# A written start-up order for fused attention and feed-forward: two rows of six sequences in the second tile, and GpSimd as a third engine in the weights' conversion

## The chip, the cores and the metric

The kernel runs on one core of a Trainium2 chip. The metric is the device time of one execution in microseconds (us). The core has a matrix engine (TensorE, PE in the profile, its weight loads PEld), VectorE (DVE), ScalarE (ACT), GpSimd (POOL) and SyncE (SP), whose queue issues the DMAs here.

## The reference

Eight sequences of 576 tokens go through attention with eight heads of 64 channels, and the joined heads through a feed-forward layer. Four heads see the last 32 tokens (local), the other four see every 32nd token before their own (strided).

```python
scores = scale * np.matmul(q, k.transpose(0, 1, 3, 2))
mask_local = (rel >= 0) & (rel < stride)
mask_strided = (rel >= 0) & (pos[None, :] % stride == pos[:, None] % stride)
attn = np.exp(scores - max); attn = attn / (sum + 1e-09)
x = matmul(attn, v)                      # (4608 tokens, 512)
h = x @ w_in                             # 512 -> 2048
return (0.5 * h * (1.0 + erf(h * inv_sqrt2))) @ w_out   # 2048 -> 512
```

## The kernel before, in words

**Tiles and steps.** The 4608 tokens are twelve tiles of 384 tokens, that is twelve rows of 32 tokens each. VISITS (L39) lists in which order rows of which sequence fill the tiles: an entry is (sequence, first row, last row). Tile 0 is rows 0 to 11 of sequence 0; tile 1 is rows 0 to 3 of sequences 1, 2 and 3. For each tile the feed-forward part has sixteen steps, one for each block of 128 hidden channels: ffn_h (L614) multiplies x by the block of w_in, twelve matmuls into H; ffn_g (L624) takes Gelu on ScalarE, rounds the result to a high part gh on ScalarE and forms the rest gl on VectorE; ffn_o (L647) multiplies by the block of w_out, nine matmuls into three accumulators O. Each product is computed as three, from operands split into a high and a low part: xh and xl, gh and gl, and the two halves of w. Steps 0 to 15 are tile 0, step 16 is the first of tile 1; there are 192.

**Weights.** Each of the 16 blocks of both weight matrices arrives as 64-bit numbers and is converted once (split_w, L141), in five instructions of 128x1024 elements, each of which may stand elsewhere in the order: the leading bits to a buffer lead (L154 on VectorE for the weights in TOP_V, L156 on ScalarE for the others), these as an integer word (L159, ScalarE), shift and OR with the rest (L161, VectorE), the high part (L165 on VectorE for those in HIGH_V, L167 on ScalarE), and the low part by subtraction (L169, VectorE). There is one buffer lead. Weights and staging share 17 slots of one pool, and a load waits until the third load before it has landed (L136).

**Local heads.** A job is 128 tokens of four heads; three jobs fill a tile. The first three jobs (local_job, L240) use dense masks; each quotient stands on VectorE (L229) for the jobs in QUOT_V and on ScalarE (L232) for the other. All others are band jobs (band_job, L282): scores (L297, 32 matmuls), maximum (L311), exponential (L315), sum and quotient and a 32x32 transpose (L318 to L321), eight DMAs of 16 KB into a band tile (L326), values (L337, 16 matmuls), and the split into xh (L236) and xl (L238).

**Strided heads.** Tile 0's strided part is done with matmuls: half_tile (two halves a and b, L375) and strided_tile (A, L418). Its operands are loaded by S and B (load_a L357, load_b L370); load_a also clears a tile p on GpSimd (L363), into which VectorE then writes. For all later tiles VectorE does it in pairs of a query row and a key row, in units of up to four rows: one L494 for each score, one L534 or L536 for each weighted value, and eight instructions for each unit (L502, L503, L520, L526, L527, L524, the transpose L544 and the split L238), besides one exponential on ScalarE (L504) and a clearing of the scores on GpSimd (L487). Tile 1 has 30 pairs in three units. load_strided (L459) loads q, k and v of a group of visits; here the three sequences of tile 1 are three DMAs each.

**What sets the order.** START (L48) is a written order up to the steady part. An entry is a job and stands for its next part: c is a weight's conversion (five parts), f a step (H, Gelu, gh, gl, O), L a local job (eleven parts, band jobs seven), a, b and A the strided part of tile 0, u1 that of tile 1 in groups of eight instructions; w, q, v, S, B, E and e are loads. Within START (L780) VectorE, ScalarE, TensorE and SP follow the written order:

```python
    with tc.manual_schedule(engines={ET.DVE, ET.Activation, ET.PE, ET.SP}):
        for it in START:
```

GpSimd's order is left to the framework's scheduler, here and later. In the steady part step(n) (L850) writes one step after the other, and run_strided (L688) deals out VectorE's strided work by a running sum of costs (0.137 a score, 0.196 a value, 0.6 a unit's end) against the due time of each tile. At thirteen steps into a tile there is a visit (L829): the values of the next tile's three band jobs (48 matmuls L337) and then the scores of the three jobs of the tile after that (96 matmuls L297), in one go. Nine visits have both, those with the values of tiles 2 to 10:

```python
    FIRST, VISIT = 2, 13
    value_at = {ready[t - 1] + VISIT: t for t in range(2, NTILE)}
    score_at = {ready[1] + FIRST: 2, **{n: t + 1 for n, t in value_at.items()}}
```

Before START, GpSimd builds the masks (mask, mask0, three masks bmask for the band jobs, L720 to L737), an identity and three cleared band tiles (L746).

Of the kernel before, what the change touches and what calls it, by code (L numbers as in the profile page):

```python
# [82 lines left out]
def attn_ffn_kernel(ctx: ExitStack, tc: tile.TileContext, qk, vl, qka, va, qs, ks, vs, w, out):  # L83
# [30 lines left out]
    smask = const.tile([P, MA], F32, name="smask")  # L114
    mask = const.tile([P, LK], F32, name="mask")
    mask0 = const.tile([P, LK], F32, name="mask0")

    bmask = {i: const.tile([P, 2 * STRIDE], F32, name=f"bmask{i}") for i in (None, 0, 1)}
# [830 lines left out]
```

## Time and profile before

| what | value |
|---|---|
| median of 3 runs | 876.04 us (874.67 to 878.77) |
| the profiled execution, own time | 877.5 us |
| its span, first to last instruction | 875.7 us |
| TensorE busy | 856.4 us (98%) |
| VectorE busy | 706.2 us (81%) |
| ScalarE busy | 482.7 us (55%) |
| GpSimd busy | 17.5 us (2%) |
| DMA | 66.67 MB, 76 GB/s in the mean |
| mean granted TensorE clock | 0.990 of full speed |

The profile is of one execution. Busy time of TensorE counts overlapping matmuls as one stretch, so what it lacks to 100% is time in which no matmul ran; the granted clock says at which share of its full speed TensorE was let run. Time lines count from the first instruction. In a time line a row gives start, length, engine, line, operation, output and inputs, and in brackets the idle time of the engine before it with what ended that; rows with a count (x) join neighbours of one kind.

### The profile page before, as it was taken

To read this page: it belongs to the slowest core of one execution; us is meant where nothing else is said; L and a number is where in the kernel's file an instruction comes from. 1 tells how busy PE (TensorE), PEld (TensorE's weight loads), DVE (VectorE), ACT (ScalarE), POOL (GpSimd) and SP (SyncE) were. 2 spreads that over 40 slices of the span, in tenths; PEclk is the share of its full clock that TensorE was granted. 3 is DMA by queue.
4 is the path that set the end of the run, shared out by engine and by line. 5 is a ranking of instruction groups with operands and counts; after the bars stand their busy time and mean duration, and the time that the engine had idled before them with its cause. 6 is when DMAs were issued, how large, how long until landed. Compare 5 with 4: busy or idle time off the path is not lost.

```text
span 875.7 us, 19634 instructions
## 1 busy us (share of the span) xinstructions
PE 856.4 (98%) x6082; PEld 771.0 (88%) x6082; DVE 706.2 (81%) x4901; ACT 482.7 (55%) x1001; POOL 17.5 (2%) x89
## 2 busy tenths in 40 slices
PE   5999999999999999999999999999999989999998
PEld 4888898999999999999999899989989979989997
DVE  6998999998989997889999979899799993751111
ACT  7888585566465375357355445556547435443222
POOL 5000100000000000000000000000000000000000
PEclk9799999999999999999999999999999999999999
DMA  9695301320310320310311121131032002000001
GB/s 352 223 380 200 115 24 37 108 76 8 128 47 9 101 97 10 104 44 8 97 50 58 55 76 47 34 122 48 9 101 80 12 30 59 18 6 12 26 1 37
DMA packets 34552, 66.67 MB, mean 76 GB/s; under 512 B 6800, under 2 KB 16528, under 8 KB 34448
## 3 DMA queue, kind: packets, MB, share of 16 engines
q1 hardware_dynamic: 34448, 65.43, 22.1%
q8 instruction: 48, 0.79, 0.4%
q14 instruction: 56, 0.46, 0.2%
HBM read 51.64 MB, written 9.44 MB: 70 GB/s over the span
## 4 chain that ended last, share of the span: by engine, by line
PE 90%; DVE 3%; DMA 3%; ACT 2%; SPq 1%; issue 1%; DVEq 0%; ACTq 0%
PE H L619 15%; PE O L659 14%; PE O L660 14%; PE H L621 14%; PE H L620 14%; PE O L658 14%; PE X_L L337 1%; PE S L297 1%; DMA ws<-in_w_dram 1%; DMA qka<-in_qka_dram 1%; DMA sk<-in_ks_dram 1%; DVE ws L161 1%; SPq L326 1%; PE S L337 1%; DVE w L169 1%
## 5 line engine op out<-in xcount | busy, mean ns | idle before, releaser
L628 ACT ACTIVATE H<-H 128x384 f32<-128x384 f32 x192 | 91.3, 476 | 363.0 <-PE H L621 304.3
L619 PE MATMUL H<-xh,w 128*128 128x384 f32 x768 | 261.6, 341 | 1.5 <-DVE gl L632 1.4
L621 PE MATMUL H<-xh,w 128*128 128x384 f32 x768 | 260.6, 339 | 0.0
L620 PE MATMUL H<-xl,w 128*128 128x384 f32 x768 | 259.4, 338 | 0.4 <-DVE xl L238 0.4
L536 DVE SCALAR_TENSOR_TENSOR acc<-sv,sc,acc 128x64 f32<-128x64 f32 x1158 | 249.5, 275 | 0.7
L660 PE MATMUL O<-w,gl 128*128 128x512 f32 x576 | 228.3, 396 | 0.0
L659 PE MATMUL O<-w,gh 128*128 128x512 f32 x576 | 227.7, 395 | 0.0
L658 PE MATMUL O<-w,gh 128*128 128x512 f32 x576 | 224.4, 390 | 0.0
L494 DVE CUSTOM_DVE_ANT_0 junk<-sq,sk 128x64 f32<-128x64 f32 x1290 | 203.8, 217 | 3.5 <-DMA sk<-in_ks_dram 2.4
L632 DVE TENSOR_TENSOR gl<-H,gh 128x384 fp32r<-128x384 f32 x192 | 105.7, 551 | 106.0 <-ACT gh L630 105.1
L619 PEld LDWEIGHTS H<-xh,w 128*128 128x128 f32 x768 | 145.4, 189 | 11.1 <-DVE gl L632 1.7
L620 PEld LDWEIGHTS H<-xl,w 128*128 128x128 f32 x768 | 145.3, 189 | 8.5 <-DVE xl L238 0.8
L621 PEld LDWEIGHTS H<-xh,w 128*128 128x128 f32 x768 | 145.0, 189 | 0.1
L660 PEld LDWEIGHTS O<-w,gl 128*128 128x128 f32 x576 | 108.1, 188 | 23.7 <-DVE gl L632 0.6
L659 PEld LDWEIGHTS O<-w,gh 128*128 128x128 f32 x576 | 108.1, 188 | 18.2
L658 PEld LDWEIGHTS O<-w,gh 128*128 128x128 f32 x576 | 108.5, 188 | 17.3
L494 DVE DVE_READ_ACCUMULATOR2_ANT sc<- 128x1 f32 x1290 | 103.6, 80 | 0.0
L630 ACT CAST gh<-H 128x384 fp32r<-128x384 f32 x192 | 92.2, 480 | 6.1
L628 ACT ACT_TABLE_LOAD x60 | 77.0, 1283 | 1.0
L504 ACT ACT_TABLE_LOAD x35 | 44.9, 1283 | 0.6
L315 ACT ACTIVATE PT_L<-P_L,nm_L 128x64 f32<-128x64 f32 x132 | 44.2, 337 | 0.3
L315 ACT ACT_TABLE_LOAD x24 | 30.8, 1283 | 0.5
(114 smaller groups left out, 488.7 us busy)
## 6 DMA issues: line engine op xcount, KB each, us to landing
ws<-in_w_dram SPq DMA_DIRECT2D x16, 1023.8 KB, 10.1
qk<-in_qk_dram SPq DMA_DIRECT2D x36, 320.0 KB, 5.0
out_dram<-ob SPq DMA_DIRECT2D x34, 256.0 KB, 2.4
vl<-in_vl_dram SPq DMA_DIRECT2D x36, 192.0 KB, 4.3
sk<-in_ks_dram SPq DMA_DIRECT2D x8, 576.0 KB, 5.5
sv<-in_vs_dram SPq DMA_DIRECT2D x8, 576.0 KB, 3.9
band<-PT_L SPq DMA_DIRECT2D x240, 16.0 KB, 1.8
sq<-in_qs_dram SPq DMA_DIRECT2D x4, 576.0 KB, 4.4
```

The costliest lines, as they stand in the source:

```text
L315: nc.scalar.activation(pv[:, :, h, :], p1[:, h * 2 * QB:(h + 1) * 2 * QB].rearrange("p (c t) -> p c t", c=2), AF.Exp, bias=nm[:, h:h + 1], ...
L494: nc.vector.tensor_tensor_reduce(junk, sq[vi, "q"][:, r0 + r, :], sq[vi, "k"][:, c, :], 1.0, 0.0, ALU.mult, ALU.add, ss[u][:, r, c:c + 1])
L536: nc.vector.scalar_tensor_tensor(acc[:, r, :], sq[vi, "v"][:, c, :], wgt, acc[:, r, :], ALU.mult, ALU.add)
L619: nc.tensor.matmul(hp, w1[f][:, 0, c, :], xh[:, c, :], start=(c == 0), stop=False)
L620: nc.tensor.matmul(hp, w1[f][:, 0, c, :], xl[:, c, :], start=False, stop=False)
L621: nc.tensor.matmul(hp, w1[f][:, 1, c, :], xh[:, c, :], start=False, stop=(c == NC - 1))
L628: nc.scalar.activation(hp, hp, AF.Gelu)
L630: nc.scalar.copy(gh, hp)
L632: nc.vector.tensor_tensor(gl, hp, gh.bitcast(F32), ALU.subtract)
L658: nc.tensor.matmul(o, gh[:, sl], w2[f][:, 0, :], start=(f == 0), stop=False)
L659: nc.tensor.matmul(o, gh[:, sl], w2[f][:, 1, :], start=False, stop=False)
L660: nc.tensor.matmul(o, gl[:, sl], w2[f][:, 0, :], start=False, stop=(f == NF - 1))
```

## The change

- VISITS: tile 1 is now rows 0 and 1 of sequences 1 to 6, two by two; sequence 7 follows whole, then rows 2 to 17 of sequences 1 to 6, then the rest of sequence 0. A unit may now hold two rows each of two sequences (units, pairs); tile 1 has 18 pairs in three units, and the tiles after it have 1272 pairs in 40 units instead of 1260 in 37.
- load_strided: a group of several sequences is one DMA for each of q, k and v. A band mask for two first rows takes the place of one of the three.
- split_w: five words (WORD_P) and five high parts (HIGH_P) go to GpSimd; VectorE takes four leading bits instead of one and three high parts instead of eight; lead has two buffers. The quotients of jobs 0 and 1 go to ScalarE (QUOT_V is empty).
- START is another order, and GpSimd follows it too.
- LATE: the scores of tiles 6 and 11 are written two steps after the visits to which they belonged.
- mask, mask0, smask and zero lie in unused columns of the slot pbig.

```diff
-VISITS = [(0, 0, 12), (1, 0, 4), (2, 0, 4), (3, 0, 4), (4, 0, 18), (5, 0, 18), (6, 0, 18), (7, 0, 18),
-          (1, 4, 18), (2, 4, 18), (3, 4, 18), (0, 12, 18)]
+VISITS = [(0, 0, 12), *[(b, 0, 2) for b in range(1, 7)], (7, 0, 18), *[(b, 2, 18) for b in range(1, 7)],
+          (0, 12, 18)]
...
 NB = 16
 START = """
-    q0 q2 S0 q1 v0 w0 B0 w1 L0 w3 L2 L0 L0 L2 L2 L0 a0 L0 L0 b0 a0 L2 a0 L0 L2 a0 L1 L2 b0 b0 b0 L0 L1
-    L2 a0 L0 b0 a0 L1 b0 a0 b0 w2 a0 b0 a0 q5 b0 L0 a0 v2 L1 L2 b0 L0 v1 c0 L1 a0 q4 L1 b0 c0 L1 A0 L1
-    c0 A0 w5 A0 c1 c0 A0 c0 c1 A0 c3 L5 c1 c3 L2 L5 L1 c2 v5 c1 w6 L4 c3 w4 L1 L2 c2 L1 L2 L4 f0 L5 w7
-    c2 L4 c1 c2 f0 f1 L5 c2 f0 c5 f0 L4 c5 f0 c3 f1 c5 f1 f2 c4 f1 c4 c5 c3 f1 f2 f2 c4 c7 L5 f2 c4 c5
-    f3 L5 w8 c7 c4 w9 E f2 f3 L5 c6 f3 c7 c6 f4 f3 c7 c6 w12 f3 c7 f4 f4 c8 c6 f5 w10 f4 c8 v3 c6 q3 w11
-    c9 c8 f4 f5 u1 f5 c9 f6 f5 w13 u1 c8 v4 c9 f5 c12 w15 c8 f6 e f6 f7 c12 u1 c9 f6 c12 f6 f7 f7 c9 w14
-    c10 f8 f7 c12 u1 c10 c12 f7 f8 c10 c11 f9 u1 c11 c10 f8 c13 c11 L4 L3 f9 f8 f9 c10 f8 c13 f9 c11 c13
-    f10 c14 c11 c14 L3 f9 c13 f10 c14 f10 L4 f11 u1 f10 c13 L3 f10 L4 u1 f11 L3 f12 u1 f11 c14 f11 u1
-    f13 f12 f12 c15 c14 f11 f13 f12 f13 u1 c15 f14 f13 u1 f12 f14 c15 f14 f14 c15 L3 u1 f13 L3 c15 u1 L3
-    f15 u1 f14 f15 f15 f15 f15 f15
+    q0 S0 q2 q1 v0 B0 w0 L0 L0 L0 b0 a0 L0 b0 L0 b0 L2 L0 a0 b0 a0 L1 b0 a0 b0 a0 L0 L2 a0 L0 b0 a0 L2
+    b0 L0 a0 b0 a0 b0 L1 v3 a0 L0 q3 b0 v1 L1 a0 w1 L2 L0 q4 c0 A0 v2 w2 L1 A0 c0 L2 w7 L1 A0 L1 c0 L2
+    L1 L3 L1 c0 A0 L2 c0 w3 L1 q5 L2 A0 c1 L2 L1 c1 L3 L2 L1 L3 L4 L2 w4 c1 e f0 c2 c1 L4 w5 c2 c1 L4 c2
+    f0 f1 w6 L3 c2 f0 L4 c3 L5 f1 f0 f1 c2 f0 c3 f1 c7 c4 c3 f2 c4 c7 c3 c4 f1 f2 c3 c4 c7 f2 f3 c5 f2
+    c4 c6 c5 f2 f3 L5 f3 c5 c6 f4 w8 f3 L5 w9 c6 w10 v4 f3 c5 c6 c5 f4 L3 c6 f5 w11 f4 L3 f4 c7 L5 f4 c8
+    c7 f5 c8 L3 f5 f6 c9 f5 c8 c9 L4 c8 f6 f7 c9 f6 L4 c10 c8 c9 f5 w12 c10 E f6 L4 w13 c11 c10 w14 f8
+    f7 c9 f7 c10 f6 f7 f8 w15 c10 f8 v5 c11 f8 f9 c12 c11 c12 f7 u1 f9 f9 c11 c12 f10 c13 f9 c11 c13 f8
+    u1 c12 f10 f10 c13 c14 f11 f10 c14 c12 f9 f11 c14 c15 c13 u1 c15 L5 f10 L5 c15 f11 u1 L5 c13 f12 f11
+    c14 u1 f11 f12 c14 u1 f13 f12 c15 f12 u1 f12 f13 f13 c15 f14 f13 u1 f13 f14 u1 f14 u1 f14 f15 u1 f14
+    f15 f15 f15 f15 f15
 """.split()
-TOP_V = [6]
-HIGH_V = [0, 1, 2, 3, 5, 6, 10, 13]
-QUOT_V = (0, 1)
+TOP_V = [0, 2, 4, 12]
+HIGH_V = [0, 5, 8]
+WORD_P = [1, 2, 5, 7, 8]
+HIGH_P = [2, 6, 9, 12, 13]
+QUOT_V = ()
...
 def units(most):
     res = []
     for k, (vi, b, r) in enumerate(ROWS):
-        if res and res[-1][0] == vi and k % TR and res[-1][3] < most:
+        n = VISITS[vi][2] if VISITS[vi][1] == 0 and VISITS[vi][2] <= most // 2 else 0
+        if res and k % TR and res[-1][3] < most and (res[-1][0] == vi or n and res[-1][6] == n):
             res[-1][3] += 1
         else:
-            res.append([vi, b, r, 1, k // TR, k % TR])
-    return res
+            res.append([vi, b, r, 1, k // TR, k % TR, n])
+    return [(*x[:6], x[6] or x[3]) for x in res]
+def pairs(u):
+    _, _, r0, nr, _, _, per = PLACE[u]
+    return [(c, r) for c in range(r0 + per) for r in range(nr) if r0 + r % per >= c]
 PLACE = units(UR)
...
         raw = wst.pop(f)
         word, other = [raw.bitcast(U32).rearrange("p (n two) -> p n two", two=2)[:, :, i] for i in range(2)]
         hf = word.bitcast(F32)
-        lead = lpool.tile([P, 2 * DM], F16, name=f"lead_{f}", tag="lead", bufs=1)
+        lead = lpool.tile([P, 2 * DM], F16, name=f"lead_{f}", tag="lead", bufs=2)
         top = raw.bitcast(BF16).rearrange("p (n four) -> p n four", four=4)[:, :, 2]
         if f in TOP_V:
             nc.vector.tensor_copy(lead, top)
...
             nc.scalar.copy(lead, top)
         yield
-        nc.scalar.activation(other.bitcast(I32), lead.bitcast(I16), AF.Copy, scale=65536.0)
+        if f in WORD_P:
+            nc.gpsimd.tensor_scalar(other.bitcast(I32), lead.bitcast(I16), 65536.0, None, ALU.mult)
+        else:
+            nc.scalar.activation(other.bitcast(I32), lead.bitcast(I16), AF.Copy, scale=65536.0)
         yield
         nc.vector.scalar_tensor_tensor(word, word, 13, other, ALU.logical_shift_right, ALU.bitwise_or)
         yield
         wt = slot(f"w_{f}", [P, 2, 2 * DM], F32R)
         if f in HIGH_V:
             nc.vector.tensor_copy(wt[:, 0, :], hf)
+        elif f in HIGH_P:
+            nc.gpsimd.tensor_copy(wt[:, 0, :], hf)
         else:
             nc.scalar.copy(wt[:, 0, :], hf)
         yield
         nc.vector.tensor_tensor(wt[:, 1, :], hf, wt[:, 0, :].bitcast(F32), ALU.subtract)
         w1[f] = wt[:, :, 0:DM].rearrange("p t (c f) -> p t c f", c=NC)
         w2[f] = wt[:, :, DM:]
+    pbig = slot("pbig", [P, 4 * DM])
+    rest = [pbig[:, i * 2 * DM + 4 * LK + DM:(i + 1) * 2 * DM] for i in range(2)]
+    pbig = [pbig[:, i * 2 * DM:(i + 1) * 2 * DM] for i in range(2)]
+    mask, mask0 = [r[:, 0:LK] for r in rest]
+    smask, zero = rest[0][:, LK:LK + MA], rest[1][:, LK:LK + 32]
     xt = {}
...
         src = {"q": qs, "k": ks, "v": vs}[nm]
         t = spool.tile([P, NR, D], F32, name=f"s{nm}_{gr}", tag=f"s{nm}", bufs=1)
         for vi in first_of[gr]:
-            b, r0, r1 = VISITS[vi]
-            o = groups[vi][1]
-            sq[vi, nm] = t[:, o:o + r1]
-            if nm != "q":
-                r0 = 0
-            nc.sync.dma_start(t[:, o + r0:o + r1], src[b, :, r0:r1])
+            sq[vi, nm] = t[:, groups[vi][1]:]
+        b, r0, r1 = VISITS[gr]
+        n = len(first_of[gr])
+        assert [VISITS[vi] for vi in first_of[gr]] == [(b + i, r0, r1) for i in range(n)] and (n == 1 or r0 == 0)
+        if nm != "q":
+            r0 = 0
+        nc.sync.dma_start(t[:, r0:n * r1].rearrange("p (b r) d -> p b (r d)", b=n),
+                          src[b:b + n, :, r0:r1].rearrange("b p r d -> p b (r d)"))
     ss = {}
     exps, splits = [], []
...
             nc.gpsimd.memset(s[:, :, 0:W], NEG)
             ss[u] = s
         ops.append((0.0, init))
-        for c in range(W):
-            for r in range(max(0, c - r0), nr):
-                def f(r=r, c=c):
-                    junk = spool.tile([P, D], F32, name=f"junk_{u}_{r}_{c}", tag="junk", bufs=4)
-                    nc.vector.tensor_tensor_reduce(
-                        junk, sq[vi, "q"][:, r0 + r, :], sq[vi, "k"][:, c, :], 1.0, 0.0,
-                        ALU.mult, ALU.add, ss[u][:, r, c:c + 1])
-                ops.append((0.137, f))
+        for c, r in pairs(u):
+            def f(r=r, c=c):
+                junk = spool.tile([P, D], F32, name=f"junk_{u}_{r}_{c}", tag="junk", bufs=4)
+                nc.vector.tensor_tensor_reduce(
+                    junk, sq[vi, "q"][:, r0 + r, :], sq[vi, "k"][:, r // per * per + c, :], 1.0, 0.0,
+                    ALU.mult, ALU.add, ss[u][:, r, c:c + 1])
+            ops.append((0.137, f))
         def sm():
             s = ss[u][:, :, 0:W]
...
     ET = mybir.EngineType
     running = {}
-    with tc.manual_schedule(engines={ET.DVE, ET.Activation, ET.PE, ET.SP}):
+    with tc.manual_schedule(engines={ET.DVE, ET.Activation, ET.PE, ET.SP, ET.Pool}):
...
-    FIRST, VISIT = 2, 13
+    FIRST, VISIT, LATE = 2, 13, (6, 11)
     value_at = {ready[t - 1] + VISIT: t for t in range(2, NTILE)}
-    score_at = {ready[1] + FIRST: 2, **{n: t + 1 for n, t in value_at.items()}}
+    score_at = {ready[1] + FIRST: 2, **{n + 2 * (t + 1 in LATE): t + 1 for n, t in value_at.items()}}
     soft_at = {}
     for n, t in score_at.items():
         for i in range(JPT if t < NTILE else 0):
...
     def visit(n):
         t = value_at.get(n, 0)
-        if score_at.get(n, 0):
-            banks[score_at[n]] = score_banks(score_at[n])
+        new = t + 1 if t else score_at.get(n, 0)
+        if new and new not in banks:
+            banks[new] = score_banks(new)
         for i in range(JPT if t else 0):
             part(t * JPT + i, 4)
         for i in range(JPT if score_at.get(n, NTILE) < NTILE else 0):
```

## Rows read from the trace of the kernel before

**Rows 1.** Busy us of each engine from 160 to 700 us (x instructions), clock, DMA

```profile
160.00:700.00 540.00, 540.00 (x3619) 488.13 (x3618) 492.34 (x3744) 303.20 (x640) 3.68 (x27) 1.00 0.18 58
```

**Rows 2.** TensorE in order of time, from the start to step 16

```profile
22.86 0.68 PE L297 MATMUL S<-qk 64*32 64x64 f32 x32 [4.50 <-DMA qk<-in_qk_dram]
...
27.61 0.69 PE L620 MATMUL H<-xl,w 128*128 128x384 f32 x1 [0.39 <-DVE xl L238]
...
83.88 0.44 PE L619 MATMUL H<-xh,w 128*128 128x384 f32 x1 [1.41 <-DVE gl L632]
...
99.59 0.33 PE L620 MATMUL H<-xl,w 128*128 128x384 f32 x1
```

**Rows 3.** VectorE in order of time, from the start to step 16

```profile
6.04 0.26 DVE L211 CUSTOM_DVE_ANT_0 pbig<-S_L,mask 128x96 f32<-128x96 f32 x1 [3.96 <-POOL mask L726]
...
26.81 0.75 DVE L238 TENSOR_TENSOR xl<-S_L,xh 128x256 fp32r<-128x256 f32 x2
...
28.05 1.22 DVE L161 SCALAR_TENSOR_TENSOR ws<-ws 128x1024 uint32<-128x1024 uint32 x1
29.19 1.22 DVE L169 TENSOR_TENSOR w<-ws,w 128x1024 fp32r<-128x1024 f32 x1
...
97.11 0.41 DVE L238 TENSOR_TENSOR xl<-xs,xh 128x256 fp32r<-128x256 f32 x1
```

**Rows 4.** TensorE in order of time at the visits of 641.98 and 711.82

```profile
641.98 1.15 PE L337 MATMUL X_L<-band,vl 96*64 96x64 f32 x32
...
648.91 0.33 PE L619 MATMUL H<-xh,w 128*128 128x384 f32 x1
...
711.82 1.15 PE L337 MATMUL X_L<-band,vl 96*64 96x64 f32 x32
...
717.44 0.30 PE L297 MATMUL S<-qk 64*32 64x64 f32 x4 [2.94 <-issue]
...
719.02 0.52 PE L619 MATMUL H<-xh,w 128*128 128x384 f32 x1
...
723.52 0.33 PE L619 MATMUL H<-xh,w 128*128 128x384 f32 x1
```

**Rows 5.** VectorE's groups, 6 to 100 us: busy us, mean ns, idle before

```profile
L494 DVE CUSTOM_DVE_ANT_0 junk<-sq,sk 128x64 f32<-128x64 f32 x56 | 9.1, 215 | 0.8 <-DMA sk<-in_ks_dram 0.8
...
L165 DVE CAST w<-ws 128x1024 fp32r<-128x1024 f32 x8 | 5.4, 678 | 0.0
...
L229 DVE TENSOR_TENSOR pbig<-pbig,rs_L 128x384 f32<-128x384 f32 x2 | 1.1, 552 | 0.0
...
L400 DVE TENSOR_TENSOR va<-va,Am 128x192 f32<-128x192 f32 x2 | 0.8, 382 | 0.0
...
L410 DVE TENSOR_TENSOR va<-va,Az 128x192 f32<-128x192 f32 x2 | 0.6, 350 | 0.0
```

**Rows 6.** ScalarE's group of quotients, 0 to 105 us

```profile
L232 ACT ACTIVATE P_L<-P_L,rs_L 128x96 f32<-128x96 f32 x4 | 1.2, 362 | 1.3 <-DVE rs_L L223 1.3
```

**Rows 7.** GpSimd in order of time, the clearing of p and the last masks

```profile
9.01 0.52 POOL L363 MEMSET va<- 128x512 f32 x1
...
13.44 0.29 POOL L737 MEMSET bmask<- 32x32 f32 x2
```

**Rows 8.** VectorE's groups in the steady part, 150 to 700 us

```profile
L536 DVE SCALAR_TENSOR_TENSOR acc<-sv,sc,acc 128x64 f32<-128x64 f32 x921 | 197.3, 276 | 0.6
...
L544 DVE STREAM_TRANSPOSE xs<-acc 128x256 f32<-128x256 f32 (+1 forms) x28 | 11.5, 411 | 0.4
```

**Rows 9.** GpSimd's groups over the whole span

```profile
L814 POOL MEMSET band<- 128x2048 f32 x1 | 1.8, 1811 | 2.6 <-DVE w L169 2.6
...
L726 POOL COPY mask<-mask 128x64 f32<-128x64 f32 x1 | 0.2, 237 | 0.1
```

**Rows 10.** SP's queue in order of time, the first sixteen band stores

```profile
32.30 11.02 SPq L326 DMA_DIRECT2D first<-PT_L  x16
```

More of the change, by code (lines that the diff above doesn't have):

```diff
@@ L113, in attn_ffn_kernel @@
     ident = const.tile([P, P], F32, name="ident")
[L114 to L118, printed above, removed]
+    bmask = {i: const.tile([P, 2 * STRIDE], F32, name=f"bmask{len(i)}") for i in ((), (0,), (0, 1))}
     def rows(j):
@@ L307, in band_job @@
         first_ = [a for a in range(2) if LPLACE[2 * x + a][1] == 0]
-        msk = bmask[first_[0] if first_ else None]
+        msk = bmask[tuple(first_)]
         for h in range(HL):
@@ L480, in strided_qk @@
     def strided_qk(u):
-        vi, _, r0, nr, t, k = PLACE[u]
-        W = r0 + nr
+        vi, _, r0, nr, t, k, per = PLACE[u]
+        W = r0 + per
         ops = []
@@ L508, in strided_av @@
     def strided_av(u):
-        vi, _, r0, nr, t, k = PLACE[u]
-        W = r0 + nr
+        vi, _, r0, nr, t, k, per = PLACE[u]
+        W = r0 + per
         ops = []
@@ L527, in strided_av, with f @@
                 (0.1, lambda: nc.vector.reciprocal(z, z)), (0.1, quotients)]
-        for c in range(W):
-            for r in range(max(0, c - r0), nr):
-                def f(r=r, c=c):
-                    acc = ss[u, "acc"]
-                    wgt = ss[u][:, r, c:c + 1]
-                    if c == 0:
-                        nc.vector.tensor_scalar_mul(acc[:, r, :], sq[vi, "v"][:, c, :], wgt)
-                    else:
-                        nc.vector.scalar_tensor_tensor(
-                            acc[:, r, :], sq[vi, "v"][:, c, :], wgt, acc[:, r, :], ALU.mult, ALU.add)
-                ops.append((0.196, f))
+        for c, r in pairs(u):
+            def f(r=r, c=c):
+                acc = ss[u, "acc"]
+                wgt = ss[u][:, r, c:c + 1]
+                value = sq[vi, "v"][:, r // per * per + c, :]
+                if c == 0:
+                    nc.vector.tensor_scalar_mul(acc[:, r, :], value, wgt)
+                else:
+                    nc.vector.scalar_tensor_tensor(acc[:, r, :], value, wgt, acc[:, r, :], ALU.mult, ALU.add)
+            ops.append((0.196, f))
         def fin():
@@ L568, in alternate @@
             for u, x in zip(us, ops):
-                r0, nr = PLACE[u][2:4]
-                key = [r for c in range(r0 + nr) for r in range(max(0, c - r0), nr)]
-                rows_ += [[f for k, f in zip(key, x) if k == r] for r in range(nr)]
+                key = [r for _, r in pairs(u)]
+                rows_ += [[f for k, f in zip(key, x) if k == r] for r in range(PLACE[u][3])]
             used = [-9] * len(rows_)
@@ L675, in attn_ffn_kernel @@
             if U0 <= v < NU:
-                vi, _, r0, nr, t, _ = PLACE[v]
+                vi, _, r0, nr, t, _, per = PLACE[v]
+                vi += nr // per - 1
                 strided += [(t, c, f) for c, f in what(v)]
-                if r0 + nr == VISITS[vi][2] and vi in last_of:
+                if r0 + per == VISITS[vi][2] and vi in last_of:
                     strided.append((t, 0.0, lambda g=last_of[vi], ns=names: [load_strided(g, nm) for nm in ns]))
@@ L705, in attn_ffn_kernel @@
     nc.scalar.activation(warm, warm, AF.Exp)
-    zero = const.tile([P, 32], F32, name="zero")
     nc.vector.memset(zero, 0.0)
@@ L713, in attn_ffn_kernel @@
                          start=True, stop=True, tile_position=(0, h * 32))
-    pbig = []
-    t = slot("pbig", [P, 4 * DM])
-    nc.gpsimd.memset(t[:, 0:1], 0.0)
-    pbig += [t[:, 0:2 * DM], t[:, 2 * DM:]]
     make_identity(nc, ident)
@@ L735, in attn_ffn_kernel @@
                                     fill=NEG, base=-1, channel_multiplier=-1)
-            if i is not None and g == 2 * i:
+            if g % 2 == 0 and g // 2 in i:
                 nc.gpsimd.memset(m[sl, 0:STRIDE], NEG)
```

## The prediction, on record before the changed kernel ran

> **What bounds the kernel now.** I read the busy times by stretch first. From 160 to 700 us TensorE is busy throughout, at a granted clock of 1.00, which is the 2.4 GHz level, while VectorE works 492 of the 540 us [rows 1]. So the end is set by when TensorE gets its first product of the feed-forward part and by where it pauses after that. The next view is TensorE's own order of time [rows 2]. The second product of step 0 waits for VectorE's split of x until 27.61. From there to step 16, the first of the steady part at 99.59, the matrix work is dense except for one wait of 1.41 us at 83.88, for VectorE's split of an earlier step. The third view is VectorE's order of time [rows 3]: its first work waits for a mask of GpSimd until 6.04, the split that releases step 0 starts at 26.81 (two instructions, 27.56 at the end), and the last split of tile 1 ends at 97.5, 2.1 us ahead of step 16. So the start is VectorE's, 91.5 us from 6.04 to 97.5. The fourth view is a pair of visits, the places where TensorE does three band jobs' products in one burst [rows 4]. The visit at 641.98 is in the second step's matrix work at 648.91, after 6.93 us; the one at 711.82 only at 723.52, after 11.70. Between them lies a pause of 2.94 us inside the scores (L297), put down to nothing that the profile shows, and behind it matmuls of 0.52 us instead of 0.33, at the lower clock. It costs 11.70 - 6.93 = 4.8 us. Of nine such bursts eight show no pause; the one at 641.98 stands for them.
>
> **The change, part by part.** Durations are from one execution that took 877.5 us (span 875.7 and 1.8 around it); the median of the runs is 876.04, 1.5 lower, and the sum is carried to it at the end. A VectorE instruction starts before the one ahead has ended, so I price by the interval between starts: 1.14 for L161 and L169, which is 0.08 under the duration [rows 3], and for the others the duration less the same 0.08: 0.60 for L165 and for leading bits taken on VectorE (L154, the same size), 0.47 for L229, 0.14 for a score L494 [rows 5].
>
> *Up to step 0.* In the old order two L161 and one L165 of weights 1 and 3 and two quotients L229 stand ahead of x's last split on VectorE. In the new one they stand behind it or, the quotients, on ScalarE; weight 0's leading bits come ahead. That is 2 x 1.14 + 0.60 + 2 x 0.47 - 0.60 = 3.2 us less in the queue that ends at 27.56. ScalarE's queue does not take its place: it gains eight quotients of 0.36 [rows 6], 2.9 us, and five conversions of whole weights leave it (weight 0's leading bits, weight 1's word, three of weights 2 and 3). On TensorE a wait goes: the scores of band job 5 stood in front of the values of jobs 2 and 1 and waited 4.50 us for their data, until 22.86 [rows 2]. Now band job 3 stands there, and its q and v are sent ahead of weight 1 instead of behind weight 10. What is late next is VectorE, as before. On SP's queue the strided data (S0) move up one place and weight 0 goes behind B0; its first instruction stands no earlier in its engine's order than it did. Against it all stands GpSimd's queue, which now follows the written order: if the clearing of p (L363, at 9.01) came behind the masks, which end at 13.7 [rows 7], VectorE's queue would wait some 4 us, and the gain would be gone. So the bounds are 0 and 4.5, the wait on TensorE. I take 3.0, by the queue: in the old trace that clearing stands between the masks.
>
> *From step 0 to step 16.* The 1.41 us wait goes with the order that made it. But ahead of the split that releases step 0's output matmuls VectorE now has one L161, leading bits and the rest of one band softmax more, and one L165 and one L169 less: 1.14 and 0.60 cancel, and the softmax stays, four instructions, the longest a transpose as long as L544's 0.41 [rows 8], 1.6 at most. I set +1.4 against -1.4: 0. Does VectorE keep up to step 16? Tile 1 falls from 30 pairs to 18: twelve scores of 0.14 and twelve values of 0.20 (0.276 less 0.08) [rows 5, 8], 4.1 us. Five L165 go and three leading bits come, -1.2; the quotients are -0.9. So its 91.5 us become 85.3, waits unchanged, and it is done at 91.3, where TensorE asks for it at 97.5 - 3.0 = 94.5. There are 3.2 us to spare for GpSimd.
>
> *GpSimd's ten instructions* (five words, five high parts, 128x1024). No row of this size reads. The memset of 2048 at 1.81 us, which only writes, gives 0.9 for 1024. The copy of 64 elements at 0.24, all of it put on the elements, gives 3.8; less the 0.15 of the smallest memsets [rows 7] it is 1.4 ns an element and 1.6 us with them [rows 9]. I take 1.6, from the row nearest in kind, with bounds 0.9 and 3.8. The engine has room, 16 us in 70. Behind each stands a VectorE instruction of the same weight, and behind that, if GpSimd is late, the next step's split and TensorE's output matmuls. The second buffer for leading bits lets ScalarE go on while GpSimd still reads the first; without it ScalarE would stand for those 1.6 us. Do GpSimd and VectorE hold each other up? L400, which reads two operands from SBUF beside back-to-back selects, took 0.382 in the mean; L410, the same shape with GpSimd idle, 0.350 [rows 5]. That is 0.03 each, and I count nothing. The Trainium skill says otherwise: in SBUF — State Buffer, "Who interferes with whom" gives the two engines a port pair under an exclusive lock, and "SBUF: two separate sides" extends it to VectorE instructions with two SBUF inputs against a GpSimd instruction that reads SBUF. By it ten times 1.6 us would be held from VectorE, 16 in the sum instead of 0; L400's rows don't show it, but the selects beside them are short.
>
> *The steady part.* The twelve pairs come back here, 4.1 us, and three more units, each with eight small instructions of at most 0.41 [rows 8], 9.8: 13.9 at most against 47.7 us in which VectorE is idle between 160 and 700 [rows 1]. Cost 0; with that cover gone, up to 13.9. Six more table loads at most fall to ScalarE, idle 237 us there.
>
> *Visits.* The scores of tiles 6 and 11 come two steps after the values of tiles 5 and 10. The second of these is the burst that pauses: 48 products stay, 96 move some 8 us away. I take the pause to be gone, -4.8; bounds -4.8 and, if it comes in two other bursts, +4.8. The Trainium skill's Runtime: NRT & Kernel Launch, "Instruction fetch mechanics", has instructions fetched in blocks of 256; 144 products with a weight load each are 288, and neither part of a split burst fills a block, by which the pause would go here. No row shows a fetch.
>
> *SP.* Nine strided loads become three. The band stores take 0.69 us each [rows 10]; sixteen still stand ahead of weight 8, the last eight move behind weight 11. Hidden by the weights already loaded; if not, ScalarE waits for weight 12 by up to eight of them, 5.5.
>
> **Sum.** 877.5 - 3.0 + 0 + 0 - 4.8 = 869.7 for the profiled execution, 868.2 at the median of 876.04.
>
> **Rivals.** *The pause stays or moves*, so that the late scores miss their aim: seven bursts are still whole, and their place among the instructions may shift. For it: one in nine paused without a visible cause. Against: eight did not, and little changes between them. It gives 876.04 - 3.0 = 873.0. *The start gains nothing*, because p is cleared late or GpSimd's results come up to 6 us late in all, with the pause gone: 876.04 - 4.8 = 871.2, and less or more by some 3. *GpSimd holds VectorE up for its whole time* between steps 1 and 16: ten times 1.6, less the 3.2 to spare, is 12.8 later, and 876.04 + 12.8 - 3.0 - 4.8 = 881.0; at 3.8 each it would be 903. It decides from 15.4 us of holding. Against it speak L400's 0.03 us; for it, that no row shows a long instruction of both at once. This is what the lock rule of the Trainium skill would give.
>
> **How the numbers follow.** Forecast 0.50, pause elsewhere 0.22, start gains nothing 0.18, GpSimd holds VectorE 0.10. A measurement here can tell about 0.5%, 4.4 us, from no change: faster is below 871.7, slower above 880.4. The forecast lies below 871.7, and so does a third of the second rival: 0.56. The last rival is slower: 0.10. The rest, 0.34, is within. The range runs from 865.0 (a start gain of 4.5 and no new wait at step 0's output, 1.5 and 1.4 below the sum) to 877.0, past the two middle rivals; that leaves out the last and a little on either side.
>
> **What would show it.** Step 0's second product near 24.6 and step 16 near 96.6; no wait of over a microsecond between them but one at step 0's output; ten GpSimd rows near 1.6 us; L161 and L169 still at 1.2 us beside them (2 or more would be the lock); no L297 row with a pause. It is wrong if step 16 begins after 99.6, if a pause of 3 us stands in another visit, or if TensorE waits for VectorE after 160 us.

## The result, and the profile after

The changed kernel took 879.81 us in the median (878.68 to 881.0, 22 runs), the kernel before beside it 876.52 (873.26 to 881.45, 22 runs): a ratio of 1.0035, 95% interval 1.0026 to 1.0045. The prediction was 868.2 and its range ended at 877.0. The first lines of the page:

```profile
span 878.2 us, 19687 instructions
## 1 busy us (share of the span) xinstructions
PE 861.3 (98%) x6082; PEld 772.8 (88%) x6082; DVE 711.7 (81%) x4921; ACT 482.3 (55%) x1011; POOL 41.1 (5%) x102
```

The span grew by 2.5 us, from 875.7. TensorE in order of time, the answer to [rows 2, 4]:

```profile
24.41 0.58 PE L290 MATMUL S_L<-pbig,vl 96*64 96x64 f32 x5 [1.55 <-issue]
26.34 0.87 PE L318 MATMUL S<-qk 64*32 64x64 f32 x32 [0.38 <-PE S_L L290]
...
27.62 0.52 PE L641 MATMUL H<-xl,w 128*128 128x384 f32 x1
...
37.03 0.50 PE L681 MATMUL O<-w,gl 128*128 128x512 f32 x1 [2.51 <-DVE gl L653]
...
105.13 0.33 PE L640 MATMUL H<-xh,w 128*128 128x384 f32 x1
...
717.99 1.15 PE L358 MATMUL X_L<-band,vl 96*64 96x64 f32 x32
...
728.11 1.12 PE L318 MATMUL S<-qk 64*32 64x64 f32 x92
...
788.37 1.15 PE L358 MATMUL X_L<-band,vl 96*64 96x64 f32 x32
```

Step 0's second product comes at 27.62, where it was at 27.61. Step 16 comes at 105.13, 5.5 us later than at 99.59 [rows 2]. The pause is gone: seven intervals between visits are 69.82 us, and the two in which the scores come late (717.99 to 788.37, and 368.31 to 438.70) are 70.39, 0.57 more each; these two are called split visits here. In the trace of before the interval with the pause was 74.60 (711.82 to 786.42). So the account of the two spans is 5.5 for the start, -4.8 for the pause, 1.1 for the two split visits. Of the 0.6 that is left, 0.5 stands behind the start of the last visit, from which the end is 89.79 us away instead of 89.30; its cause was not followed.

What happened up to step 16 is seen on VectorE, GpSimd and SP's queue, each in order of time [rows 3, 7, 10]:

```profile
10.60 0.36 DVE L417 TENSOR_TENSOR va<-A,pbig 128x192 f32<-128x192 f32 x1 [2.48 <-POOL va L384]
...
26.30 0.75 DVE L259 TENSOR_TENSOR xl<-S_L,xh 128x256 fp32r<-128x256 f32 x2
...
33.68 1.17 DVE L341 TENSOR_TENSOR PT_L<-PT_L,rs_L 128x256 f32<-128x256 f32 x1
...
72.91 0.69 DVE L162 CAST lead<-ws 128x1024 f16<-128x1024 bf16 x1 [3.49 <-DMA ws<-in_w_dram]
...
79.94 1.14 DVE L517 CUSTOM_DVE_ANT_0 junk<-sq,sk 128x64 f32<-128x64 f32 x1
```

```profile
6.40 2.19 POOL L749 TENSOR_SCALAR_AFFINE_SELECT bmask<-bmask 32x64 f32<-32x64 f32 x8
...
10.04 0.52 POOL L384 MEMSET va<- 128x512 f32 x1
...
24.16 3.12 POOL L168 TENSOR_SCALAR ws<-lead 128x1024 int32<-128x1024 int16 x1 [10.78 <-ACT lead L164]
...
33.42 1.14 POOL L178 CAST w<-ws 128x1024 fp32r<-128x1024 f32 x1 [1.33 <-DVE ws L172]
...
79.86 1.14 POOL L178 CAST w<-ws 128x1024 fp32r<-128x1024 f32 x1 [14.65 <-DVE w L182]
```

```profile
35.40 11.36 SPq L347 DMA_DIRECT2D first<-PT_L  x16
46.81 1.53 SPq L142 DMA_DIRECT2D ws<-in_w_dram  x3
...
58.09 5.73 SPq L347 DMA_DIRECT2D first<-PT_L  x8
...
65.01 0.37 SPq L142 DMA_DIRECT2D ws<-in_w_dram  x1
```

Three things are to be seen. p is cleared at 10.04 instead of 9.01, behind eight selects and three fills, and VectorE waits 2.48 us for it. Two VectorE instructions end just behind a GpSimd copy that ran beside them (by 0.29 and 0.08 us): L341 takes 1.17 instead of 0.42 and a score L517 takes 1.14 instead of 0.22. And weights 8, 9 and 10 are sent only behind sixteen band stores, weight 12 behind eight more, and VectorE waits 3.49 us for weight 12. A fourth is in TensorE's rows: it pauses 1.55 us at 24.41 inside the values of a local job, for nothing that the profile shows.

### The profile page after: what moved, and what is told of

The parts are those of the page before. It is cut to its first block, busy times and chain, and to the rows that moved or that the text cites. A ratio compares the mean times of both kernels' runs of the same rounds, so it can differ in the third digit from the quotient of the medians.

```text
span 878.2 us, 19687 instructions
## 1 busy us (share of the span) xinstructions
PE 861.3 (98%) x6082; PEld 772.8 (88%) x6082; DVE 711.7 (81%) x4921; ACT 482.3 (55%) x1011; POOL 41.1 (5%) x102
## 4 chain that ended last, share of the span: by engine, by line
PE 88%; POOL 3%; DVE 3%; issue 3%; ACT 2%; DMA 1%; POOLq 0%; SPq 0%; ACTq 0%; DVEq 0%
PE H L640 14%; PE O L681 14%; PE O L680 14%; PE H L642 14%; PE H L641 14%; PE O L679 14%; POOL ws L168 2%; PE S L318 1%; PE X_L L358 1%; DMA sk<-in_ks_dram 1%; DVE ws L172 1%; PE S L358 1%; DVE junk L517 0%; DVE w L182 0%; POOL w L178 0%
## 5 line engine op out<-in xcount | busy, mean ns | idle before, releaser
L559 DVE SCALAR_TENSOR_TENSOR acc<-sv,sc,acc 128x64 f32<-128x64 f32 x1158 | 247.4, 278 | 1.0
L517 DVE CUSTOM_DVE_ANT_0 junk<-sq,sk 128x64 f32<-128x64 f32 x1290 | 204.3, 219 | 6.8 <-DMA sk<-in_ks_dram 6.6
L517 DVE DVE_READ_ACCUMULATOR2_ANT sc<- 128x1 f32 x1290 | 105.4, 82 | 0.0
L511 POOL MEMSET sc<- 128x64 f32 (+7 forms) x40 | 5.1, 131 | 627.4 <-DVE acc L559 627.2
```

Of the source, the lines that this page charges most:

```text
L517: nc.vector.tensor_tensor_reduce(junk, sq[vi, "q"][:, r0 + r, :], sq[vi, "k"][:, r // per * per + c, :], 1.0, 0.0, ALU.mult, ALU.add, ss[u ...
L559: nc.vector.scalar_tensor_tensor(acc[:, r, :], value, wgt, acc[:, r, :], ALU.mult, ALU.add)
```

## The experiments

Each ratio is to the kernel before, run beside it on the same chip; the median of before lay between 876.4 and 877.2 there. The changed kernel was not run again beside the versions, so a difference between its median and theirs carries that scatter too. "Step 16" is its time in the one profiled execution. Three profiled executions have the changed START with nothing altered before step 16 (the changed kernel, the one without `LATE`, and the one with extra GpSimd instructions): step 0 begins at 27.13, 26.17 and 27.11, step 16 at 105.13, 105.31 and 105.16. So step 16 repeats within 0.2 us in these three, though step 0 moves by 1.0.

**Is the pause worth 4.8 us?** The kernel before with `LATE` alone, and the changed kernel without it:

```diff
-    FIRST, VISIT = 2, 13
+    FIRST, VISIT, LATE = 2, 13, (6, 11)
...
-    score_at = {ready[1] + FIRST: 2, **{n: t + 1 for n, t in value_at.items()}}
+    score_at = {ready[1] + FIRST: 2, **{n + 2 * (t + 1 in LATE): t + 1 for n, t in value_at.items()}}
...
```

> The kernel before with LATE alone. Theory (the pause of 4.77 us in the scores of the visit at 711.82 goes when the scores come two steps later, and each such split visit costs 0.57 us, as the changed kernel's trace shows): 876.5 - 4.8 + 1.1 = 872.8, step 16 still at 99.6, and runs that lie within about 1.5 us of each other as those of the changed kernel do. Rival (the pause comes in another burst): 876.5 + 1.1 = 877.6 with a pause of some 5 us in another visit.

Measured: 877.39 us, ratio 1.0005 (0.9991 to 1.002), nothing gained. The theory's 872.8 failed; the time is the rival's, but no other visit has a pause of 5 us. Its step 16 came at 101.70, with the same START as before. The visit at 717 has no pause any more, but 2.6 us beyond the two splits were lost in other intervals, 1.2 of them in a wait of TensorE for VectorE's gl.

```diff
-    FIRST, VISIT, LATE = 2, 13, (6, 11)
+    FIRST, VISIT, LATE = 2, 13, ()
```

> The changed kernel with LATE empty. Theory (the pause belongs to a whole burst at that place of the program): a pause of 4.8 us in one visit and 0.57 less in each of two, 879.8 + 4.8 - 1.1 = 883.5, with runs that scatter more. Rival (the pause belonged to the old order or to its alignment): 878.7 and no pause.

Measured: 878.97 us, ratio 1.0022 (1.0008 to 1.0037), all nine intervals 69.80 to 69.83, so no pause in whole bursts. The rival held. In the new kernel `LATE` has no pause to remove and costs 0.8 us in the median (1.1 in the intervals between visits); the intervals of the two ratios overlap.

**Does the kernel before have a fixed start and a fixed pause?** It was profiled a second time, unchanged.

> The kernel before, unchanged, in a second profiled execution. Theory (its start and its pauses differ from execution to execution, as its runs from 873.3 to 881.5 do): step 16 between 99.6 and 102, and a pause other than 4.8 us, or none, at the visit near 712. Rival (both belong to the program): step 16 within 0.3 us of 99.6 and the same pause there.

TensorE's order of time in this second execution (877.13 us):

```profile
24.92 0.68 PE L297 MATMUL S<-qk 64*32 64x64 f32 x32 [3.96 <-DMA qk<-in_qk_dram]
...
102.44 0.33 PE L620 MATMUL H<-xl,w 128*128 128x384 f32 x1
...
718.64 0.30 PE L297 MATMUL S<-qk 64*32 64x64 f32 x4 [0.85 <-issue]
```

Step 16 came 2.9 us later than in the execution on which the prediction rests, and the pause at the same burst was 0.85 instead of 2.94. What the nine intervals lost against 69.83 is 1.6 us here and 4.8 there, so step 16 and the loss together give 104.0 and 104.4. The changed kernel's 105.13 + 1.1 + 0.6 is 106.8, 2.4 to 2.8 above these; the medians differ by 3.3. The theory held, with a step 16 that came 0.4 us later than its range: the prediction's base joined an early start with a long pause. The late start was there at step 0 already, whose second product came at 30.05 instead of 27.61, so against this execution the changed kernel's step 0 is 2.4 us early.

**GpSimd's part.** First its ten instructions went to ScalarE:

```diff
-WORD_P = [1, 2, 5, 7, 8]
-HIGH_P = [2, 6, 9, 12, 13]
+WORD_P = []
+HIGH_P = []
```

> The changed kernel with the five words and the five high parts on ScalarE. Theory (GpSimd makes the start late: VectorE waited 3.2 us for words and its instructions on two SBUF operands were some 6 us longer beside GpSimd's): step 16 some 5 us earlier than 105.1, near 100, and 875; no VectorE row of L182, L341 or L517 longer than it is alone. Rival (the written order, the late clearing of p and weight 12 make it late, and ScalarE, with ten times 1.14 us more, becomes the next to wait for): step 16 at 105 or later, 880 to 886.

Measured: 880.33 us, ratio 1.0039 (1.0024 to 1.0054), step 16 at 104.38. The theory (near 100, and 875) failed, and the time is the rival's: what TensorE waited for moved to ScalarE, as its groups of waits up to 112 us show (line waited for: us in total, times, longest):

```profile
PE O L679 <- ACT gh L651: 2.3, 2, 1.9
```

Then only the high parts were moved, to VectorE:

```diff
-HIGH_V = [0, 5, 8]
-HIGH_P = [2, 6, 9, 12, 13]
+HIGH_V = [0, 2, 5, 6, 8, 9, 12, 13]
+HIGH_P = []
```

> The changed kernel with the five high parts of GpSimd on VectorE. Theory (a GpSimd copy holds VectorE's instructions on two SBUF operands for all of its 1.14 us, which is more than the 0.69 that VectorE takes for the same copy): step 16 no later than 105.1, by up to 2 us sooner, 878 to 880. Rival (GpSimd takes work off VectorE): five times 0.6 us later, step 16 near 108, 882.8.

Measured: 878.64 us, ratio 1.0005 (0.999 to 1.0021), step 16 at 103.68. VectorE got five copies more, some 3 us, and step 16 came 1.45 us sooner. VectorE's order of time shows why:

```profile
29.63 1.59 DVE L182 TENSOR_TENSOR w<-ws,w 128x1024 fp32r<-128x1024 f32 x1
33.53 0.42 DVE L341 TENSOR_TENSOR PT_L<-PT_L,rs_L 128x256 f32<-128x256 f32 x1
...
53.84 2.36 DVE L182 TENSOR_TENSOR w<-ws,w 128x1024 fp32r<-128x1024 f32 x2
```

The theory held. L341 is back from 1.17 to 0.42, and the two L182 that took 3.15 beside a copy take 2.36. The L182 beside a word (29.63) is still 0.37 longer than the 1.22 that it takes alone.

What GpSimd does to VectorE by itself was measured with extra instructions on a scratch tile:

```diff
+        k = {3: 1, 5: 2, 7: 3}.get(n // NF)
+        if k == 1:
+            nc.gpsimd.tensor_copy(sb.bitcast(F32), sa.bitcast(F32))
+        elif k == 2:
+            nc.gpsimd.tensor_scalar(sb.bitcast(I32), sa.bitcast(I16)[:, 0:DM], 65536.0, None, ALU.mult)
+        elif k == 3:
+            nc.gpsimd.memset(sb.bitcast(F32), 0.0)
```

> The changed kernel with one extra GpSimd instruction of 128x512 at each step of tile 3 (copy of f32), tile 5 (word from int16) and tile 7 (fill, which reads nothing), on a scratch tile of its own. Theory (GpSimd and VectorE hold each other where both move f32 between SBUF tiles): beside a copy a VectorE score L517 or value L559 is longer by what is left of the copy, some 0.5 us, a gl L653 that reads PSUM is not; beside a word the lengthening is smaller; beside a fill none. Rival (they do not hold each other): the means of L517, L559 and L653 are the same in the four stretches within 3%.

GpSimd waits for nothing here and ran far ahead of the steps: the copies stand between 86 and 123 us, twelve of the words from 136.4 to 155.3, the fills from 163.5 to 172.8. VectorE in order of time beside nine copies in a row (0.61 to 0.75 us each), two neighbouring scores:

```profile
100.08 0.62 DVE L517 CUSTOM_DVE_ANT_0 junk<-sq,sk 128x64 f32<-128x64 f32 x1
...
100.63 0.21 DVE L517 CUSTOM_DVE_ANT_0 junk<-sq,sk 128x64 f32<-128x64 f32 x1
```

VectorE's groups from 136.5 to 155.2, beside the words (1.50 us each), and then from 155.4 to 163.3, beside nothing:

```profile
L517 DVE CUSTOM_DVE_ANT_0 junk<-sq,sk 128x64 f32<-128x64 f32 x39 | 9.3, 259 | 0.0
...
L559 DVE SCALAR_TENSOR_TENSOR acc<-sv,sc,acc 128x64 f32<-128x64 f32 x23 | 7.5, 342 | 0.0
...
L653 DVE TENSOR_TENSOR gl<-H,gh 128x384 fp32r<-128x384 f32 x4 | 2.2, 549 | 0.0
```

```profile
L517 DVE CUSTOM_DVE_ANT_0 junk<-sq,sk 128x64 f32<-128x64 f32 x21 | 4.3, 218 | 0.0
...
L559 DVE SCALAR_TENSOR_TENSOR acc<-sv,sc,acc 128x64 f32<-128x64 f32 x15 | 4.2, 278 | 0.0
...
L653 DVE TENSOR_TENSOR gl<-H,gh 128x384 fp32r<-128x384 f32 x3 | 1.7, 553 | 0.0
```

Scores and values, whose operands lie in SBUF, are held up: by some 0.4 us where a copy holds one, and by some 0.4 for each word too, though that takes 1.50. gl, which reads PSUM, is not (549 against 553). Beside the fills L517 took 220 and L559 277, as alone. The theory held for all three, and the execution took 890.7 us.

Two rows of the changed kernel's own trace go further. A copy that begins while VectorE is at a two-operand instruction is itself late, and a fill can hold another VectorE instruction: L557, a product of a tile with one number for each row, ends with the fill and takes 1.00 instead of 0.25. VectorE and GpSimd, in order of time:

```profile
84.47 1.21 DVE L172 SCALAR_TENSOR_TENSOR ws<-ws 128x1024 uint32<-128x1024 uint32 x1
...
97.86 1.00 DVE L557 TENSOR_SCALAR acc<-sv,sc 128x64 f32<-128x64 f32 x1
```

```profile
84.61 2.05 POOL L178 CAST w<-ws 128x1024 fp32r<-128x1024 f32 x1 [3.62 <-DVE w L182]
...
97.00 1.81 POOL L832 MEMSET band<- 128x2048 f32 x1 [1.39 <-PE O L681]
```

The copy at 84.61 ends 0.98 us behind the end of that L172.

**The tile alone.** The old START (three groups of u1 fewer), the old choice of engines and one buffer lead, with the new VISITS, and GpSimd left to the scheduler:

```diff
-    q0 S0 q2 q1 v0 B0 w0 L0 L0 L0 b0 a0 L0 b0 L0 b0 L2 L0 a0 b0 a0 L1 b0 a0 b0 a0 L0 L2 a0 L0 b0 a0 L2
...
+    q0 q2 S0 q1 v0 w0 B0 w1 L0 w3 L2 L0 L0 L2 L2 L0 a0 L0 L0 b0 a0 L2 a0 L0 L2 a0 L1 L2 b0 b0 b0 L0 L1
...
...
-WORD_P = [1, 2, 5, 7, 8]
-HIGH_P = [2, 6, 9, 12, 13]
...
+WORD_P = []
+HIGH_P = []
...
```

> The changed kernel's VISITS, LATE and loads with the old START (three groups of tile 1 fewer), its old choice of engines, one buffer lead, and GpSimd left to the scheduler. Theory (the tile is harmless, the new order and GpSimd cost the start): step 16 at 99.6 or up to 2 earlier, since VectorE has 4 us less to do, and 870 to 873. Rival (the new tile costs the start, for example by its larger loads): step 16 after 101, 875 or more.

Measured: 884.89 us, ratio 1.009 (1.0071 to 1.0109), the slowest, with step 16 at 111.33. By its numbers the rival's condition is met, but it doesn't settle what the tile costs: with other groups in u1, the work of tile 1 stands elsewhere among VectorE's instructions. Part of the loss is a wait of TensorE for a gl behind it (order of time):

```profile
94.05 0.44 PE L640 MATMUL H<-xh,w 128*128 128x384 f32 x1 [3.40 <-DVE gl L653]
```

From 26 us on TensorE waited 8.6 us for gl and gh in all, and VectorE 7.7 for ScalarE's words instead of 3.1 in the kernel before. What the new tile costs with an order of its own is not shown.

**The clearing of p.** The masks of the band jobs and the three cleared band tiles are built behind S0:

```diff
...
+                if kind == "S":
+                    masks()
...
```

> The changed kernel, with the masks of the band jobs and the cleared band tiles built behind the clearing of p instead of ahead of it. Theory (the late clearing took the start's gain): VectorE's first work on p (L417) no longer waits until 10.6, step 0's second product comes some 2.5 us sooner, near 25.1, step 16 as much sooner, near 102.6, and 877.3. Rival (what comes behind step 0, the weights and GpSimd's words, sets step 16 anyway): the second product sooner, step 16 within 0.7 us of 105.1, 879 to 880.

GpSimd's clearing, VectorE's first work on p and step 0 on TensorE, each in order of time:

```profile
2.21 0.52 POOL L384 MEMSET va<- 128x512 f32 x1
```

```profile
7.54 0.36 DVE L417 TENSOR_TENSOR va<-A,pbig 128x192 f32<-128x192 f32 x1
```

```profile
24.88 0.69 PE L640 MATMUL H<-xh,w 128*128 128x384 f32 x1
```

Measured: 878.41 us, ratio 1.0012 (0.9994 to 1.0031). Step 0 began at 24.88 instead of 27.13, step 16 at 103.19, 1.94 sooner. So the theory held in this execution, nearly in its size (2.5). In the median it is 1.4 us, and the interval overlaps with the changed kernel's (1.0026 to 1.0045).

**SP's order.** Weights 8, 9 and 10 ahead of the band stores, weight 12 ahead of the last eight:

```diff
-    f0 f1 w6 L3 c2 f0 L4 c3 L5 f1 f0 f1 c2 f0 c3 f1 c7 c4 c3 f2 c4 c7 c3 c4 f1 f2 c3 c4 c7 f2 f3 c5 f2
-    c4 c6 c5 f2 f3 L5 f3 c5 c6 f4 w8 f3 L5 w9 c6 w10 v4 f3 c5 c6 c5 f4 L3 c6 f5 w11 f4 L3 f4 c7 L5 f4 c8
-    c7 f5 c8 L3 f5 f6 c9 f5 c8 c9 L4 c8 f6 f7 c9 f6 L4 c10 c8 c9 f5 w12 c10 E f6 L4 w13 c11 c10 w14 f8
+    f0 f1 w6 w8 w9 L3 c2 f0 w10 L4 c3 L5 f1 f0 f1 c2 f0 c3 f1 c7 c4 c3 f2 c4 c7 c3 c4 f1 f2 c3 c4 c7 f2 f3 c5 f2
+    c4 c6 c5 f2 f3 L5 f3 c5 c6 f4 f3 L5 c6 v4 f3 c5 c6 c5 f4 L3 c6 f5 w11 w12 f4 L3 f4 c7 L5 f4 c8
+    c7 f5 c8 L3 f5 f6 c9 f5 c8 c9 L4 c8 f6 f7 c9 f6 L4 c10 c8 c9 f5 c10 E f6 L4 w13 c11 c10 w14 f8
```

> The changed kernel with the loads of weights 8, 9 and 10 ahead of the sixteen band stores and weight 12 ahead of the last eight. Theory (SP's stores hold the weights up): the DMA engines no longer stand at 77 GB/s between 40 and 50 us, VectorE's wait of 3.49 us for weight 12 and ScalarE's of 3.78 behind it are gone, step 16 some 3 us sooner, near 102, 877. Rival (the weights come in time and VectorE with GpSimd is what is late): those waits move to another place, step 16 within 0.7 us of 105.1, 879 to 880.5.

SP's queue in order of time, and step 16 on TensorE:

```profile
27.18 9.93 SPq L142 DMA_DIRECT2D ws<-in_w_dram  x4
37.22 8.14 SPq L347 DMA_DIRECT2D first<-PT_L  x8
```

```profile
101.49 0.33 PE L640 MATMUL H<-xh,w 128*128 128x384 f32 x1
```

Measured: 876.46 us, ratio 0.9985 (0.997 to 1.0001). From 40 to 50 us the DMA engines moved 215 GB/s instead of 77, VectorE's wait of 3.49 us is gone, and step 16 came 3.64 sooner. The theory held; this is the largest single cost. The edit moves weights 8 to 10 ahead of the first sixteen stores too, where the kernel before has them behind, so it may be worth more than undoing the change at weight 12 alone, which was not run.

**Do they add up?** `LATE` empty, p cleared first, the high parts on VectorE, and the weights ahead of the stores, together:

> The changed kernel with four edits together: LATE empty, p cleared first, the high parts on VectorE, weights 8 to 12 ahead of the band stores. Theory (four separate costs, measured alone as 0.8, 1.4, 1.2 and 3.3 us): they add up to 6.7, 879.8 - 6.7 = 873.1, step 16 near 99. Rival (one queue after the other: three of them shorten the same stretch, and the largest hides the rest): 879.8 - 3.3 - 0.8 = 875.7, step 16 near 101.

Measured: 874.35 us, ratio 0.9965 (0.995 to 0.998), 5.5 below the changed kernel. Step 16 was at 101.12, 4.0 sooner, where the three start edits alone had made 1.94 + 1.45 + 3.64 = 7.0. The total lies between the theory and the rival. TensorE in order of time shows where most of the missing 3.0 stands:

```profile
8.77 0.52 PE L408 MATMUL A<-qka 64*32 64x24 f32 x19 [0.86 <-issue]
...
27.10 0.69 PE L640 MATMUL H<-xh,w 128*128 128x384 f32 x1
...
101.12 0.33 PE L640 MATMUL H<-xh,w 128*128 128x384 f32 x1
```

Step 0 began at 27.10, as late as in the changed kernel, though p was cleared at 2.22: TensorE paused 0.86 us in the scores of tile 0's strided part, for nothing that the profile shows, where the run with p alone has no such pause. From step 0 to 16 the three edits alone had taken -0.31, 1.32 and 3.49 us off the changed kernel's 78.0, 4.5 in all, and together they took 4.0. So that the edits share a stretch, as the rival said, is not shown; but an earlier step 0 does not always move step 16 (26.17 and 105.31 above), and it stays open how much of the sum can be had.

Two more edits on top of these, the first moving step 0's gl ahead of both band softmaxes, the second all words to ScalarE as well:

```diff
-    f0 f1 w6 w8 w9 L3 c2 f0 w10 L4 c3 L5 f1 f0 f1 c2 f0 c3 f1 c7 c4 c3 f2 c4 c7 c3 c4 f1 f2 c3 c4 c7 f2 f3 c5 f2
+    f0 f1 w6 w8 w9 f0 c2 f0 L3 w10 L4 c3 L5 f1 f1 c2 f0 c3 f1 c7 c4 c3 f2 c4 c7 c3 c4 f1 f2 c3 c4 c7 f2 f3 c5 f2
```

> The four edits and step 0's gl ahead of the two band softmaxes on VectorE. Theory (TensorE's 2.5 us at step 0's output are lost for good): 2 us less than the four edits. Rival (VectorE has the same work to do and the next weight's split is late instead): within 0.7 us of the four edits.

Measured: 874.08 us, ratio 0.9964 (0.9948 to 0.9979): nothing gained, as the rival said. TensorE's wait of over 2 us at step 0's output is down to 0.5, but its groups of waits up to 106 us show it again one work further, at the low parts of the weights:

```profile
PE H L642 <- DVE w L182: 2.8, 4, 1.3
```

> The same with the five words on ScalarE, so that GpSimd takes no part in the conversion. Theory (words of 3.1 us on GpSimd cost more than they save): 1 to 2 us less than the kernel with step 0's gl first. Rival (ScalarE, with 5 times 1.14 us more, is late with gh and the leading bits): 1 us more or the same.

Measured: 873.85 us, ratio 0.9959 (0.9945 to 0.9973): the same within the interval, so the theory failed and the words can stand on either engine. In this version GpSimd converts nothing; it is faster than both kernels, against the one before by 0.4% by the ratio and 0.3% by the medians (873.85 and 876.39).

## Why the prediction was wrong

In the two profiles the forecast of 869.7 is missed by 10.2 us. Step 16 was to begin near 96.6 and began at 105.13: that is 8.5. The two split visits cost 1.1, and 0.6 is left, as said above. So it is the start that failed, by four terms; a fifth, the visits, failed in the median. (By its own terms the range's lower end is 865.3, not 865.0; nothing hangs on it.)

**Up to step 0** (-3.0, measured 0; -2.4 against the second execution of the kernel before). The step that failed: "I take 3.0, by the queue: in the old trace that clearing stands between the masks." In the written order it stands behind eight selects and the fills, at 10.04, and VectorE waits 2.48 us. The prediction had named this ("the gain would be gone") and gave it, with GpSimd's results coming late, a chance of 0.18. It was to be foreseen without a row: the masks are written ahead of START, and GpSimd now follows the text. Yet the clearing is only 1.0 us later than before. VectorE is free at 8.12, so at its old place, until 9.53, the clearing would still have held it some 1.4 us, by an estimate from these rows: a shorter queue gains nothing ahead of a wait. The size of 3.0 is not shown either. With the clearing first, step 0 begins 2.25, 0.03, 1.92 and 0.56 us sooner in the four profiled versions that have it; in the second and fourth TensorE pauses 0.86 and 0.74 us near 8 us, and why is open.

**SP** (0 taken; putting the loads first gained 3.3 us in the median, 3.64 at step 16). "Hidden by the weights already loaded; if not, ScalarE waits for weight 12 by up to eight of them, 5.5" failed in its first half. The wait for weight 12, 3.49 us on VectorE, lies within the bound. Sixteen stores stand ahead of weight 8 in both orders; what differs is the last eight. The second execution of the kernel before has on SP's queue, in order of time:

```profile
66.38 0.33 SPq L134 DMA_DIRECT2D ws<-in_w_dram  x1
85.15 4.95 SPq L326 DMA_DIRECT2D first<-PT_L  x8
```

There the stores follow the last weight; in the changed kernel weights 12 to 15 are sent behind them, at 65.01 and from 70.46 on.

**GpSimd's instructions** (no hold counted). "That is 0.03 each, and I count nothing" failed: L400 stood beside selects of 32 partitions that take 0.27 us, and says nothing of long copies. In the trace after, the VectorE rows beside the four copies that held it are 0.75, 0.79, 0.92 and 0.91 us longer than alone, 3.4 in all, those beside words (five rows) some 2.3, and VectorE waits 3.2 for words. The durations lay within the bounds of 0.9 and 3.8: the copies took 1.14 to 2.05, 1.57 in the mean, as the 1.6 taken, but the words 3.13, twice that. VectorE makes the same copy in 0.69: four of the five copies given to GpSimd cost VectorE more than making them. The Trainium skill, in SBUF — State Buffer, "SBUF: two separate sides", has an exclusive lock between a GpSimd instruction that reads SBUF and a VectorE instruction with two SBUF inputs, and this is the rule that the prediction weighed and set aside. The trace agrees on which instructions are held and on copies; it disagrees where the Trainium skill says that the lock lasts for the whole instruction, since a word of 1.50 us held a score for some 0.4. The rival built on that rule stood at 881.0 with a chance of 0.10; 879.8 came near it, but by three causes, of which the hold is not the largest: taking the copies off GpSimd was worth 1.2 us in the median.

**From step 0 to 16** (0). "There are 3.2 us to spare for GpSimd" counted VectorE's work and left its waits unchanged; the late weights and the words are waits. The +1.4 for step 0's output was in truth 2.51 on TensorE, and behind it the granted clock was 0.50, the 1.2 GHz level, from 38.2 to 41.4 us, for which there was no term; what that costs at step 16 no run separates. Moving that gl forward gained nothing. With the faults mended, step 16 came at 101.12, 100.26 and 100.69 in the last three versions, 3.7 us or more behind 96.6, while the old START had it at 99.59, 101.70 and 102.44 in three profiled executions. So a gain of the new order at step 16 is not shown, and what sets step 16 there stays open. That these versions take 2.0 to 2.5 us less than the kernel before goes with their visits, whose nine intervals are 69.83 to 69.92 without a pause.

**Visits** (-4.8). In the two profiles compared it holds, less 1.1 for the two splits. It failed as a term of the median: "Of nine such bursts eight show no pause" was read as a fixed cost at one place, from one execution. A second one had 0.85 there and a start 2.9 us later, and `LATE` in the old kernel gained nothing. The prediction's reading of the Trainium skill's Runtime: NRT & Kernel Launch, "Instruction fetch mechanics", by which a whole burst pauses because it fills a block of 256 instructions, is not borne out: nine whole bursts in the changed kernel without `LATE` show no pause. The Trainium skill itself calls the cost of crossing such a block mostly hidden. What causes the pause in the old kernel stays open.

**Right**: the 4.50 us wait of the scores at 22.86 is gone (0.38 at 26.34), though TensorE now pauses 1.55 us at 24.41 (the second execution of the kernel before has a pause of 0.92 at the like place). The steady part hides its three extra units: every interval without a split is as long as before. ScalarE's table loads, 123 instead of 119 before Gelu, exponentials and band exponentials, show in no interval either.

## What to carry to other kernels

Where an engine begins to follow a written order, everything written ahead of that order moves ahead too: look first at what another engine waits for there. On a queue that issues both loads and small stores, price a store by the load behind it. Copies between SBUF tiles given to GpSimd should be charged to VectorE as well, unless VectorE reads PSUM meanwhile, as gl did here; and a base for a prediction should be read from two executions where the runs scatter by 1%.
